# Products of one-query attention issued in register-addressed loops instead of written out

## The chip, the cores and the metric

One NeuronCore of a Trainium2 chip runs the whole program. The time is device microseconds of one execution, taken as the median of three executions. A profile of one execution gives the span from the first to the last instruction and the records that the text below reads.

## The reference, cut to what matters

One token attends to 65,536 cached positions in 16 heads of 256 values; a small gated layer multiplies the result. All tensors are bf16.

```python
# x (1,1,448); k_cache, v_cache (1,16,65536,256); wq (448,4096); wo (4096,448); w1 (448,1792); w2 (1792,448)
xn = layernorm(x)
q = (xn @ wq).reshape(1, 1, 16, 256).transpose(0, 2, 1, 3)
scores = einsum("bhqd,bhkd->bhqk", q, k_cache) * 256 ** -0.5
p = softmax(scores)
o = einsum("bhqk,bhkd->bhqd", p, v_cache)
s = o.transpose(0, 2, 1, 3).reshape(1, 1, 4096) @ wo
g = silu(silu(xn @ w1) @ w2)
out = x + s * g
```

Keys and values together are 1,074 MB; each byte is used once.

## The kernel before, in words

**Blocks and buffers.** The cache is cut into 64 blocks (`NBLK`), four for each head. A block is 16,384 positions: 128 partitions, each with `KB` = 128 positions of 256 values, 8.39 MB. Three such buffers in SBUF (`R[0]` to `R[2]`, one tensor `RR`) hold keys and values in turn: slot `s` takes the keys of block i, then the values of block i, then the keys of block i + 3. SyncE's queue (SP) issues all loads in the order keys(i), values(i - 1), keys(i + 1), values(i), and so on. In `load_k` (L227) it first takes the semaphores `vh[s]` and `vf[s]`, which TensorE raises when the values in that slot have been multiplied, half and whole; in `load_v` (L233) it takes `kf[s]`, which VectorE raises when the keys in that slot have been used.

**Scores.** VectorE (`dve_block`) multiplies the keys by the query and sums part of the products itself; ScalarE (`act_sums`, L331) sums the other part, 18 of each 32 positions, in four steps for a block (`SUB` = 32). VectorE's `end` needs both. It copies the scores (L261) and takes the maximum of each partition (L262, semaphore `rm`).

**Values.** TensorE runs `pe_block` for each block: `pe_turn` (turns the previous result, needs `oc`), `pe_max` (maximum over partitions, next query, broadcast: L378, L440, L384) and `pe_v` (L452), which multiplies the values of the block before that maximum's. `pe_v` accumulates 64 products of two positions each, 128 x 512 values a product (L366 in `pe_keys`), in the two rows of `psO`, and raises `od`; the one-column product of `pe_mark` (L450) then raises `vf[s]`. ScalarE, in the middle of its own next block (after two of four steps), takes `od` and copies `psO` to `O` (`act_out`, L357), which raises `oc`; a step later it stores the turned result (`act_row`, L361).

**Order at the two ends.** The first blocks wait for their data. In the last ones, block 61's values go through `pe_v_split`: 96 positions (most of them in a loop of four register-addressed products, L464 and L466), then `pe_max` of block 62, then the rest. Block 62's values come in two pieces and block 63's in three; both are multiplied by `pe_groups` (L408), which spreads the products over four pairs of rows in one PSUM bank, 32 rows apart, and needs `pe_turn_groups` (L422) and a VectorE sum (`dve_row`, L434) behind it. Between these stand the maxima of the last keys, and the output projection (`project`, L928) by pieces of `wo` that come last of all loads. The gate's second `silu` on ScalarE (L722) and VectorE (L724 to L731), the weights of the last head (L869 to L879) and the final sum over blocks (L888, L895) run on those engines in program order.

The outer TensorE loop, three blocks a pass, is written with the helper `loop`. Two queues, SP's and ScalarE's, store the two halves of the output (L1036).

Of the kernel before, what the change touches and what calls it, by code (L numbers as in the profile page):

```python
# [10 lines left out]
ET = mybir.EngineType  # L11
# [3 lines left out]
KB = 128  # L15
SUB = 32
NR = 3
# [7 lines left out]
def kernel(  # L25
# [12 lines left out]
    nc = tc.nc  # L38
    bf16 = mybir.dt.bfloat16
    fp32 = mybir.dt.float32  # L40
    P = nc.NUM_PARTITIONS

    _, _, D = A_x.shape
    _, H, Sk, Dh = A_k_cache.shape
# [4 lines left out]
    NBLK = H * NB  # L49
    assert NBLK % NR == 1 and NBLK >= 8  # L50
    LAST = NBLK - 1
# [19 lines left out]
    pe, dve, act, gp, sp = nc.tensor, nc.vector, nc.scalar, nc.gpsimd, nc.sync  # L71


    KW, HK = KB * Dh, KB // 2
# [8 lines left out]
    PVV = pool.tile([P, NR * KB], bf16, name="PV")  # L83
# [10 lines left out]
    hist = pool.tile([P, 2 + NENT, 4], fp32, name="hist")  # L94
    ident = pool.tile([P, P], bf16, name="ident")
# [28 lines left out]
    wq_t, n = rest(0, DF * HD + HD // 2)  # L124
    Z, n = rest(n, DX * HP * HP)
    w1_t, n = rest(n, DF * F + F // 2)
    w2_t, n = rest(n, FC * D)
# [35 lines left out]
    def mark(e, ins):  # L163
        count[e] += 1
        ins.then_inc(line[e], 1)
        return (e, count[e])

    def need(e, *toks):
        for p, c in toks:
            if seen.get((e, p), 0) < c:  # L170
                eng[e].wait_ge(line[p], c)
                seen[(e, p)] = c
# [4 lines left out]
    def take(e, s, k=1):  # L177
        e.wait_ge(s, k).then_inc(s, -k)  # L178
# [176 lines left out]
    def act_out(po=psO):  # L355
        take(act, od)
        act.copy(out=O[0 : po.shape[0], :], in_=po).then_inc(oc, 1)  # L357

    def act_row(e):
        take(act, ho)  # L360
        return act.copy(out=hist[:, at(e + 2), 2:4].rearrange("p o s -> p (o s)"), in_=ps_t)  # L361


    def pe_keys(po, t, s, k0, k1, start, stop, done=None):
        for c in range(k0, k1, 2):
            ins = pe.matmul(  # L366
                po,
                lhsT=PV[t][:, c : c + 2],
                rhs=R[s][:, c * Dh : (c + 2) * Dh],
                start=(start and c == k0),  # L370
                stop=(stop and c == k1 - 2),
            )
        if done is not None:
            ins.then_inc(done, 1)

    def pe_rows():
        take(pe, rm)
        pe.matmul(  # L378
            ps_m[0:1, :], lhsT=rmax[:, 0:1], rhs=ident[:, :], start=True, stop=True
        ).then_inc(tm, 1)  # L380

    def pe_bcast():
        take(pe, gm)
        pe.matmul(  # L384
            ps_nb, lhsT=ones_row[0:1, :], rhs=gmax[0:1, :], start=True, stop=True
        ).then_inc(bm, 1)
# [3 lines left out]
    def pe_turn():  # L390
        take(pe, oc)
        Ov = O[0:2, :].rearrange("r (j p a) -> r j a p", j=2, a=2)
        for a in range(2):
            for j in range(2):
                ins = pe.matmul(  # L395
                    ps_t2[:, 2 * a : 2 * a + 2],
                    lhsT=Ov[:, j, a, :],
                    rhs=eye2[:, j, :],
                    start=(j == 0),
                    stop=(j == 1),  # L400
                    is_transpose=True,
                )
        ins.then_inc(ho, 1)

    def pe_groups(po, t, s, k0, k1, first, end):
        for c in range(k0, k1, 2):
            p = PG * (c // 2 % G)
            ins = pe.matmul(  # L408
                po[p : p + 2, :],
                lhsT=PV[t][:, c : c + 2],  # L410
                rhs=R[s][:, c * Dh : (c + 2) * Dh],
                start=(c < first + 2 * G),
                stop=(c >= end - 2 * G),
            )
        return ins

    def pe_turn_groups():
        take(pe, oc)
        Ov = O[:, :].rearrange("r (j p a) -> r j a p", j=2, a=2)
        for a in range(2):  # L420
            for j in range(2):
                ins = pe.matmul(  # L422
                    ps_tg[:, a, :],
                    lhsT=Ov[:, j, a, :],
                    rhs=eye4[:, j, :],
                    start=(j == 0),
                    stop=(j == 1),
                    is_transpose=True,
                )
        return mark("pe", ins)  # L430

    def dve_row(o, t):
        need("dve", t)
        return mark("dve", dve.tensor_reduce(out=o, in_=ps_t4, axis=AX.X, op=ALU.add))  # L434
# [14 lines left out]
    def pe_mark():  # L449
        return pe.matmul(ps_z, lhsT=ident[:, 0:1], rhs=ident[:, 0:1], start=True, stop=True)  # L450

    def pe_v(s):  # L452
        take(pe, pv)
        take(pe, vl[s], 16)
        pe_keys(psO, s, s, 0, HK, True, False, vh[s])
        pe_keys(psO, s, s, HK, KB, False, True, od)
        pe_mark().then_inc(vf[s], 1)

    def pe_v_split(s, k, between):
        take(pe, pv)  # L460
        take(pe, vl[s], 16)
        n = SUB // 4
        pe_keys(psO, s, s, 0, n, True, False)
        with nc.Fori(n, k, n, engines={ET.PE}, hint_back_edge=True) as c:  # L464
            for d in range(0, n, 2):
                pe.matmul(  # L466
                    psO,
                    lhsT=PVV[:, bass.ds(c + (s * KB + d), 2)],
                    rhs=RR[:, bass.ds(c * Dh + (s * KW + d * Dh), 2 * Dh)],
                    start=False,  # L470
                    stop=False,
                )
        between()
        pe_keys(psO, s, s, k, KB, False, True, od)
        pe_mark().then_inc(vf[s], 1)


    def pe_max(i):
        pe_rows()
        pe_query(i + 1)  # L480
        pe_bcast()

    def pe_block(i, s):
        pe_turn()
        pe_max(i)
        pe_v(s)
# [4 lines left out]
    def loop(g, a, b, step, block, more=0, always=False):  # L491
        es, name = {g.engine}, f"passes_{nc.next_id()}"
        head, ann, body, rest, join, tail = (
            f"{name}_{x}" for x in ("head", "ann", "body", "rest", "join", "tail")
        )
        assert (b - a) % step == 0 and more < step
        last = b if more else b - step
        r = nc.alloc_registers(f"{name}_i", engines=es)
        nc.regs_mov(r, a)
        nc.br(head, engines=es)  # L500

        def go(lo, hi):
            i = nc.snap(r, min_val=a, max_val=last)
            for s in range(lo, hi):
                block(i + s, s)

        if always:
            with nc.body(head, valid_engines=es):
                hint = g.mark_branch_hint_location()
                nc.br(body, engines=es)  # L510
        else:
            with nc.body(head, valid_engines=es):
                g.br_eq(r, last, on_true=body, on_false=ann)
            with nc.body(ann, valid_engines=es):
                hint = g.mark_branch_hint_location()
                nc.br(body, engines=es)
        with nc.body(body, valid_engines=es):
            go(0, more or step)
            if more:
                g.br_eq(r, last, on_true=join, on_false=rest)  # L520
            else:
                nc.br(join, engines=es)
        if more:
            with nc.body(rest, valid_engines=es):
                go(more, step)
                nc.br(join, engines=es)
        with nc.body(join, valid_engines=es):
            nc.regs_alu(r, r, step, op=mybir.AluOpType.add)
            g.br_lt(r, last + 1, on_true=head, on_false=tail).branch_hint(hint)
        nc.switch_bb(tail)  # L530
# [76 lines left out]
    with tc.tile_critical(sync_engine=ET.Pool, no_gpsimd_drain=True):  # L607
# [228 lines left out]
        none(ps_t2).then_inc(ho, 1)  # L836
        need("pe", t9)
        pe_max(0)
        loop(pe, 1, NBLK - 3, NR, pe_block, more=1)
        pe_turn()  # L840
        pe_v_split(1, 96, lambda: pe_max(NBLK - 2))


        def shares(e0, e1, h0, h1):
# [115 lines left out]
        take(pe, pv)  # L960

        pe.wait_ge(nl[0], 16)
        pe_groups(ps_g, 2, 2, 0, HK, 0, KB)
        pe_rows()
        pe_bcast()
        pe_quads()
        pe.wait_ge(nl[1], 16)
        pe_groups(ps_g, 2, 2, HK, KB, 0, KB).then_inc(od, 1)
        take(pe, wy)
        pe.wait_ge(wp, 16)  # L970
        project(0, 4 * PQ)
        take(pe, pv)
        pe.wait_ge(zl[0], 16)
        pe_groups(ps_g2, 0, 1, 0, HK, 0, HK).then_inc(od, 1)
        act_out(ps_g)
        act_softmax(LAST + 1, PV[0][:, HK:KB], HK, KB)
        pe_rows()
        pe.wait_ge(wl[0], 16)
# [1 line left out]
        project(r0, r1 - 2)  # L980
        pe_bcast()
        project(r1 - 2, r1)
        t = pe_turn_groups()
        need("act", t)
        act_out(ps_g2)
        t = dve_row(hist[:, LAST + 1, 2:4], t)
        t = mark("dve", dve.memset(g_t, 0.0))
        mark("dve", dve.memset(x_t, 0.0))
        need("dve", ("dve", count["dve"]))
        for p, w in halves:  # L990
            mark("dve", dve.tensor_copy(out=x_t[p, :], in_=x_f[0:1, w]))
        t_g = silu([(g_t[p, :], w) for p, w in halves], ps_y, g_e, t_y)
        need("pe", t)
        t_x = pe_turn_groups()
        take(pe, pv)
        t15 = pe_sums(ps_m[:, 0:NL], N1, NENT)
# [5 lines left out]
        need("dve", t)  # L1002
        weights(N1, NENT, H1, H, (ps_m[:, 0:NL], t15))
        t_r = dve_row(hist[:, LAST + 2, 2:4], t_x)
        need("dve", t_r)
        outputs(N1, NENT - 1, H1, H, NL - 1)
        for n in range(1, len(vz)):
            pe.wait_ge(zl[n], 16)
# [58 lines left out]
```

## Time and profile before

| | before |
|---|---|
| median of three runs (lowest to highest) | 2513.66 us (2513.61 to 2513.69) |
| the profiled execution's own time | 2513.66 us |
| its span, first to last instruction | 2511.3 us |
| VectorE busy | 2175.9 us, 87% of the span |
| ScalarE busy | 1930.3 us, 77% |
| TensorE busy | 1129.9 us, 45% |
| moved by DMA | 1084.37 MB, 432 GB/s over the span |
| mean granted TensorE clock | 0.702 |

The profiled execution took as long as the median of the runs, so its rows can be set against the measured time directly; 2.4 us of the time lie outside the span. In the profile's lines, PE is TensorE, PEld its weight loads, DVE VectorE, ACT ScalarE and SP SyncE; a letter q behind an engine means its sequencer. L366 is a line of the kernel file. In a timeline, the columns are start in us, length in us, engine, line, operation, output from inputs and count; in brackets stands how long the engine had been idle before and what ended that.

### The profile page before, as it was taken

To read this page: it belongs to the slowest core of one execution; us is meant where nothing else is said; L and a number is where in the kernel's file an instruction comes from. 1 tells how busy PE (TensorE), PEld (TensorE's weight loads), DVE (VectorE), ACT (ScalarE), POOL (GpSimd) and SP (SyncE) were. 2 spreads that over 40 slices of the span, in tenths; PEclk is the share of its full clock that TensorE was granted. 3 is DMA by queue.
4 is the path that set the end of the run, shared out by engine and by line. 5 is a ranking of instruction groups with operands and counts; after the bars stand their busy time and mean duration, and the time that the engine had idled before them with its cause. 6 is when DMAs were issued, how large, how long until landed. Compare 5 with 4: busy or idle time off the path is not lost. (4 is left out here: it accounts for less than half of the span.)

```text
span 2511.3 us, 30167 instructions
## 1 busy us (share of the span) xinstructions
PE 1129.9 (45%) x4775; PEld 430.3 (17%) x4775; DVE 2175.9 (87%) x1573; ACT 1930.3 (77%) x9555; POOL 2.4 (0%) x17
## 2 busy tenths in 40 slices
PE   3253543534535445345354453443544534435455
PEld 1121211211112112111121121111211211112122
DVE  6979889889898898898988988989889888898898
ACT  5868778778787787787877877878778777787786
POOL 0000000000000000000000000000000000000000
PEclk7676766767667677677676776766767767677677
DMA  9999999999999999999999999999999999999999
GB/s 424 424 437 434 434 434 434 434 433 434 431 433 432 432 433 434 430 433 434 434 434 433 434 434 434 434 434 434 434 434 434 431 433 432 434 433 432 431 431 386
DMA packets 21738, 1084.37 MB, mean 432 GB/s; under 512 B 2405, under 2 KB 2918, under 8 KB 3942
## 3 DMA queue, kind: packets, MB, share of 16 engines
q1 hardware_dynamic: 21730, 1084.30, 99.9%
q8 instruction: 4, 0.07, 0.0%
q10 hardware_dynamic: 4, 0.00, 0.0%
HBM read 1084.29 MB, written 0.00 MB: 432 GB/s over the span
## 5 line engine op out<-in xcount | busy, mean ns | idle before, releaser
L331 ACT ACTIVATE R<-R x4608 | 1839.0, 400 | 368.6 <-ACTq L178 368.6
L268 DVE TENSOR_TENSOR R<-R,qcur 128x4608 bf16<-128x4608 bf16 (+1 forms) x512 | 1130.9, 2219 | 248.5 <-DVEq L178 248.4
L366 PE MATMUL bank<-R,PV 128*2 128x512 bf16 x3924 | 985.9, 418 | 13.3 <-PEq L178 5.8
L314 DVE TENSOR_REDUCE S<-R 128x13 f32<-128x3328 bf16 (+1 forms) x256 | 925.8, 3617 | 0.0
L331 ACT ACTIVATION_READ_ACCUMULATOR R<-R x4608 | 857.4, 186 | 0.0
L366 PEld LDWEIGHTS bank<-R,PV 128*2 128x2 bf16 x3924 | 351.4, 90 | 620.7 <-issue 203.5
L378 PE MATMUL bank<-ident,rmax 128*1 128x128 bf16 x65 | 17.2, 264 | 931.0 <-PEq L178 930.8
L395 PE MATMUL bank<-eye,O 2*128 2x2 f32 x252 | 38.2, 252 | 379.1 <-PEq L178 379.1
L378 PEld LDWEIGHTS bank<-ident,rmax 128*1 128x1 bf16 x65 | 5.2, 79 | 936.5 <-issue 936.5
L344 ACT ACTIVATE hist<-bank 128x1 f32 (+1 forms) x65 | 11.1, 171 | 157.5 <-ACTq L178 157.5
L302 DVE CUSTOM_DVE_ANT_0 R<-R,qcur 128x256 bf16<-128x256 bf16 x252 | 105.4, 418 | 0.0
L395 PEld LDWEIGHTS bank<-eye,O 2*128 2x128 f32 x252 | 34.6, 208 | 395.5 <-issue 395.5
L250 DVE TENSOR_REDUCE gmax<-bank 1x1 bf16<-1x128 f32 x65 | 18.3, 281 | 35.9 <-DVEq L178 35.9
L357 ACT COPY O<-bank 2x512 f32<-2x512 f32 (+1 forms) x67 | 37.5, 560 | 6.8 <-ACTq L178 6.6
L289 DVE CAST qcur<-bank 128x256 bf16<-128x256 f32 x64 | 27.2, 425 | 16.0 <-DVEq L178 15.9
L346 ACT ACTIVATE PV<-S,hist 128x128 f32 (+1 forms) x65 | 26.0, 400 | 14.7 <-ACTq L178 14.4
L440 PE MATMUL bank<-q,ident 8*128 (+1 forms) x63 | 24.3, 386 | 7.6 <-issue 1.2
L261 DVE COPY S<-S 128x128 f32<-128x128 f32 (+1 forms) x65 | 14.7, 226 | 11.7 <-DVEq L178 2.5
L408 PE MATMUL bank<-R,PV 128*2 128x512 bf16 x128 | 13.9, 604 | 15.4 <-DMA R<-in_A_v_cache_dram 15.4
L302 DVE DVE_READ_ACCUMULATOR2_ANT S<- 128x1 f32 x252 | 20.8, 82 | 0.0
L262 DVE TENSOR_REDUCE rmax<-S 128x1 bf16<-128x128 f32 (+1 forms) x65 | 18.2, 280 | 0.0
L384 PE MATMUL bank<-gmax,ones_row 1*128 1x1 bf16 x65 | 10.3, 158 | 6.9 <-PEq L178 2.9
(90 smaller groups left out, 133.8 us busy)
## 6 DMA issues: line engine op xcount, KB each, us to landing
R<-in_A_k_cache_dram SPq DMA_DIRECT2D x7, 4096.0 KB, 26.5
R<-in_A_v_cache_dram SPq DMA_DIRECT2D x3, 4096.0 KB, 24.6
R<-in_A_k_cache_dram SPq DMA_DIRECT2D x2, 2048.0 KB, 19.9
R<-in_A_wq_dram SPq DMA_DIRECT2D x1, 3072.0 KB, 12.8
R<-in_A_v_cache_dram SPq DMA_DIRECT2D x1, 3072.0 KB, 23.0
R<-in_A_wo_dram SPq DMA_DIRECT2D x4, 448.0 KB, 26.6
R<-in_B_w_dram SPq DMA_DIRECT2D x1, 1568.0 KB, 25.3
R<-in_B_w_dram SPq DMA_DIRECT2D x1, 1344.0 KB, 5.7
```

Of the source, the lines that this page charges most:

```text
L250: dve.reduce_max(out=gmax[0:1, :], in_=ps_m[0:1, :], axis=AX.X).then_inc(gm, 1)
L268: return dve.tensor_tensor(out=keys, in0=keys, in1=qcur[:, None, :].to_broadcast([P, c1 - c0, Dh]), op=ALU.mult,)
L289: dve.tensor_copy(out=qcur[:, :], in_=ps_q).then_inc(sd, 1)
L302: dve.tensor_tensor_reduce(out=Kv[:, c, :], in0=Kv[:, c, :], in1=qcur[:, :], scale=1.0, scalar=0.0, op0=ALU.mult, op1=ALU.add, accum_out=S ...
L314: ins = dve.tensor_reduce(out=S[:, c1:c2], in_=Kv[:, c1:c2, :], axis=AX.X, op=ALU.add)
L331: ins = act.activation(out=prod, in_=prod, func=ACT.Identity, accum_out=S[:, bass.ds(c0 + c, 1)],)
L346: act.activation(out=pv_out, in_=S2[:, c0:c1], func=ACT.Exp, bias=col(0, 1), scale=scale, accum_out=col(1, 2),).then_inc(pv, 1)
L357: act.copy(out=O[0 : po.shape[0], :], in_=po).then_inc(oc, 1)
L366: ins = pe.matmul(po, lhsT=PV[t][:, c : c + 2], rhs=R[s][:, c * Dh : (c + 2) * Dh], start=(start and c == k0), stop=(stop and c == k1 - 2),)
L378: pe.matmul(ps_m[0:1, :], lhsT=rmax[:, 0:1], rhs=ident[:, :], start=True, stop=True).then_inc(tm, 1)
L395: ins = pe.matmul(ps_t2[:, 2 * a : 2 * a + 2], lhsT=Ov[:, j, a, :], rhs=eye2[:, j, :], start=(j == 0), stop=(j == 1), is_transpose=True,)
L440: pe.matmul(ps_q, lhsT=ident[0:HP, at(j)].to_broadcast([HP, P]), rhs=q8[:, o : o + Dh] if isinstance(o, int) else q8[:, bass.ds(o, Dh)], s ...
```

## The change

The TensorE code for the values is rewritten. `pe_keys_loop` multiplies positions k0 to k1 in a loop of four products a pass (8 positions), with the addresses of weights and data taken from the loop's register. `pe_zero` is a product of 128 x 512 with a zero result that opens and closes the accumulation, since the products in the loop neither start nor stop it. `pe_v` is now: zero, loop over one half, a `pe_mark` that raises `vh[s]`, loop over the other half, zero, mark. Block 61 uses the same function with `pe_max` between. Block 62's values, which used `pe_groups`, now go through the loop too, in pieces of 32, 32 and 64 positions, into the two rows of `psO`; so their result is turned by `pe_turn` and stored by ScalarE's `act_row` in place of VectorE's `dve_row`. Block 63 keeps `pe_groups`. The outer loop of TensorE is an ordinary `Fori`, with one block behind it. The two stores of the output are the same in both kernels.

```diff
-    def pe_v(s):
-        take(pe, pv)
-        take(pe, vl[s], 16)
-        pe_keys(psO, s, s, 0, HK, True, False, vh[s])
-        pe_keys(psO, s, s, HK, KB, False, True, od)
-        pe_mark().then_inc(vf[s], 1)
-
-    def pe_v_split(s, k, between):
...
-        pe_keys(psO, s, s, 0, n, True, False)
-        with nc.Fori(n, k, n, engines={ET.PE}, hint_back_edge=True) as c:
+    def pe_keys_loop(t, s, k0, k1):
+        n = 8
+        with nc.Fori(k0, k1, n, engines={ET.PE}, hint_back_edge=True) as r:
+            c = nc.snap(r, min_val=k0, max_val=k1 - n)
             for d in range(0, n, 2):
                 pe.matmul(
                     psO,
-                    lhsT=PVV[:, bass.ds(c + (s * KB + d), 2)],
+                    lhsT=PVV[:, bass.ds(c + (t * KB + d), 2)],
                     rhs=RR[:, bass.ds(c * Dh + (s * KW + d * Dh), 2 * Dh)],
                     start=False,
                     stop=False,
                 )
-        between()
-        pe_keys(psO, s, s, k, KB, False, True, od)
+
+    def pe_zero(start):
+        return pe.matmul(
+            psO,
+            lhsT=ident[:, 0:2],
+            rhs=ident[:, 2:3].to_broadcast([P, 2 * Dh]),
+            start=start,
+            stop=not start,
+        )
+
+    def pe_v(s, k=HK, between=None):
+        take(pe, pv)
+        take(pe, vl[s], 16)
+        pe_zero(True)
+        pe_keys_loop(s, s, 0, k)
+        if between:
+            between()
+        else:
+            pe_mark().then_inc(vh[s], 1)
+        pe_keys_loop(s, s, k, KB)
+        pe_zero(False).then_inc(od, 1)
         pe_mark().then_inc(vf[s], 1)
...
-        loop(pe, 1, NBLK - 3, NR, pe_block, more=1)
+        with nc.Fori(1, NBLK - 3, NR, engines={ET.PE}, hint_back_edge=True) as i:
+            for s in range(NR):
+                pe_block(i + s, s)
+        pe_block(NBLK - 3, 0)
         pe_turn()
-        pe_v_split(1, 96, lambda: pe_max(NBLK - 2))
+        pe_v(1, 96, lambda: pe_max(NBLK - 2))
...
         pe.wait_ge(nl[0], 16)
-        pe_groups(ps_g, 2, 2, 0, HK, 0, KB)
+        pe_zero(True)
+        pe_keys_loop(2, 2, 0, SUB)
         pe_rows()
+        pe_keys_loop(2, 2, SUB, HK)
         pe_bcast()
         pe_quads()
         pe.wait_ge(nl[1], 16)
-        pe_groups(ps_g, 2, 2, HK, KB, 0, KB).then_inc(od, 1)
+        pe_keys_loop(2, 2, HK, KB)
+        pe_zero(False).then_inc(od, 1)
...
-        act_out(ps_g)
+        act_out()
...
-        t = pe_turn_groups()
-        need("act", t)
+        pe_turn()
+        t_a = mark("act", act_row(LAST - 1))
         act_out(ps_g2)
-        t = dve_row(hist[:, LAST + 1, 2:4], t)
...
-        need("pe", t)
+        need("pe", t_a)
         t_x = pe_turn_groups()
...
-        need("dve", t_r)
+        need("dve", t_a, t_r)
```

More of the change, by code (lines that the diff above doesn't have):

```diff
@@ L450, in pe_mark @@
         return pe.matmul(ps_z, lhsT=ident[:, 0:1], rhs=ident[:, 0:1], start=True, stop=True)
-    def pe_v(s):
-        take(pe, pv)
-        take(pe, vl[s], 16)
-        pe_keys(psO, s, s, 0, HK, True, False, vh[s])
-        pe_keys(psO, s, s, HK, KB, False, True, od)
-        pe_mark().then_inc(vf[s], 1)
-    def pe_v_split(s, k, between):
-        take(pe, pv)
-        take(pe, vl[s], 16)
-        n = SUB // 4
-        pe_keys(psO, s, s, 0, n, True, False)
-        with nc.Fori(n, k, n, engines={ET.PE}, hint_back_edge=True) as c:
+    def pe_keys_loop(t, s, k0, k1):
+        n = 8
+        with nc.Fori(k0, k1, n, engines={ET.PE}, hint_back_edge=True) as r:
+            c = nc.snap(r, min_val=k0, max_val=k1 - n)
             for d in range(0, n, 2):
```

## The prediction

> **What bounds the kernel now.** First the page: share of the DMA engines, queues, and the chain that ended last.
>
> ```profile
> DMA  9999999999999999999999999999999999999999
> ...
> q1 hardware_dynamic: 21730, 1084.30, 99.9%
> q8 instruction: 4, 0.07, 0.0%
> ...
> DMA R<-in_A_wo_dram 1%; SPq L810 0%; SPq L237 0%; PE bank L928 0%; DVE S L1031 0%; DVE S L1033 0%
> ```
>
> The 16 DMA engines never rest, and the last load ends the program. At 433 GB/s a block (16.8 MB of keys and values) takes 38.7 us, and that is the period of every engine's work. The change moves no byte, so it can cost time only where a load is issued too late or where the work after the last loads grows. Hence the second view, the timeline of one steady block:
>
> ```profile
> 2300.51 0.33 SPq L233 DMA_DIRECT2D R<-in_A_v_cache_dram  x1
> ...
> 2301.80 15.77 PE L366 MATMUL bank<-R,PV 128*2 128x512 bf16 x64 [0.21 <-PEq L178]
> ...
> 2308.68 0.42 ACT L331 ACTIVATE R<-R  x1 [5.99 <-ACTq L178]
> ...
> 2317.85 0.33 SPq L227 DMA_DIRECT2D R<-in_A_k_cache_dram  x1
> ...
> 2323.06 0.56 ACT L357 COPY O<-bank 2x512 f32<-2x512 f32 x1
> ```
>
> TensorE's 64 products (call their stretch V, first product to mark: 15.6 us here, 15.1 to 16.8 over the blocks) hold two things: the next load of keys (2317.85) and ScalarE's copy of the result (2323.06). Values issued at 2300.51 land after a median 24.6 us, at 2325.1; until then the DMA engines are busy without the keys.
>
> Third, the price of a looped product. Block 61 already runs in such a loop (timeline of TensorE, then the loop's own line):
>
> ```profile
> 2443.08 7.37 PE L466 MATMUL bank<-R,PV 128*2 x28
> 2450.68 1.02 PE L466 MATMUL bank<-R,PV 128*2 x4 [0.23 <-issue]
> 2451.87 1.02 PE L466 MATMUL bank<-R,PV 128*2 x4 [0.17 <-issue]
> 2453.12 1.02 PE L466 MATMUL bank<-R,PV 128*2 x4 [0.23 <-issue]
> 2454.37 1.02 PE L466 MATMUL bank<-R,PV 128*2 x4 [0.23 <-issue]
> ```
>
> ```profile
> L464 PEldq BRANCH_PREFETCH_HINT  x11: 31/31/35, 2441.6 to 2454.1; - x11
> ...
> L464 PEldq COMPARE_BRANCH  x11: 80/230/240, 2442.6 to 2455.0; - x11
> ```
>
> Eleven passes begin from 2441.6 to 2454.1: 1.25 us a pass. While the clock is still low (a product each 0.43 us) the array is slower than that; after it rises (0.215 us) four products take 0.86 us and the array waits for its sequencer in each pass ("issue"). So the sequencer sets the pace.
>
> **The change, part by part.** *V of blocks 0 to 60.* 16 passes x 1.25 = 20.0 us; 0.1 us to enter the first loop and 0.15 for mark and entry of the second (in the trace the wait's end to the first hint is 0.2 us, eight more instructions included); 0.2 for the closing zero. V = 20.5. The second `snap` adds a register move per pass that no row shows alone. Joined to the register instruction already there (L464, 78 ns; the smallest of this kind is 42) it costs little; alone it costs 0.1 us, as the MOVE at 2441.46 before the hint at 2441.56. I take 0.02, nearer to the joined row: 0.3 us a block, with ends 0 and 1.6. Below nothing: some passes take 1.20. So V = 20.8, between 19.7 and 22.1, or 4.9 us more than the mean of 15.9.
>
> [...] The profile shows four instruction packets in all, and the trace has none between 66 and 2434 us, while TensorE's outer loop jumped back some twenty times; so the jumps are put at nothing.
>
> *Who waits for a longer V.* Two limits.
> (a) The load of keys. From V's start (2301.80) to the landing of the values ahead (2325.1) are 23.3 us. Off go 0.45 from the mark to the issue and 1.05 from issue to first packet (the run's first DMA: issued at 0.90, first packet at 1.95). V may reach 21.8.
> (b) ScalarE. It works without a gap through its block (only the 5.99 us at its start are idle), and the copy stands in its middle. Where the copy does wait, at the start, TensorE and ScalarE make a loop of their own (timelines of TensorE and ScalarE):
>
> ```profile
> 98.71 16.50 PE L366 MATMUL bank<-R,PV 128*2 128x512 bf16 x64 [3.30 <-PEq L178]
> 115.05 0.17 PE L450 MATMUL bank<-ident 128*1 128x1 bf16 x1
> ...
> 132.38 4.85 PE L366 MATMUL bank<-R,PV 128*2 128x512 bf16 x11
> ```
>
> ```profile
> 115.33 0.57 ACT L357 COPY O<-bank 2x512 f32<-2x512 f32 x1 [2.25 <-ACTq L178]
> ```
>
> From the mark (115.05) to the next V (132.38) are 17.3 us: copy, second half of the sums, maximum, next query. So the loop needs V + 17.3 a block and fits into 38.7 while V stays below 21.4. With 20.8 both limits hold: no cost in steady state, 0.6 us to spare.
>
> *The start.* V of block 0 begins with its landing (98.71) and ends 4.4 us later than before; ScalarE, already waiting there, goes 4.3 us late, and with it VectorE and V of block 1: 136.7 instead of 132.4. Its mark comes at 157.5, the keys' issue 0.3 later (149.25 before), their first packet at 158.8; the values ahead land at 157.8 (issued 130.99, now some 4 us later, still in time). The engines rest about 1.0 us, once; block 2's V comes at 174.8 by (b), and from block 3 on the loads lead again. Ends 0 and 3.
>
> *The tail.* Timelines of ScalarE, TensorE and VectorE:
>
> ```profile
> 2460.12 0.57 ACT L357 COPY O<-bank 2x512 f32<-2x512 f32 x1 [2.55 <-ACTq L178]
> ```
>
> ```profile
> 2470.46 3.58 PE L408 MATMUL bank<-R,PV 128*2 128x512 bf16 x32 [9.02 <-DMA R<-in_A_v_cache_dram]
> 2476.22 0.27 PE L378 MATMUL bank<-ident,rmax 128*1 128x128 bf16 x1 [2.17 <-PEq L178]
> ...
> 2480.76 3.58 PE L408 MATMUL bank<-R,PV 128*2 128x512 bf16 x32
> ```
>
> ```profile
> 2496.89 2.94 DVE L728 RECIPROCAL R<-R 1x448 f32<-1x448 f32 x1
> ```
>
> - Block 61: twelve looped passes before `pe_max` (now at 2456.6, +1.3), then four: result at 2463.2 instead of 2460.0. ScalarE's copy, which already waits there, goes 3.2 later and with it all its sums of the last block, VectorE's first half (L261 at 2478.5, +2.8) and its second (rm at 2496.1, +2.8).
> - Block 62: `pe_groups` took 3.6 us for 32 products; the loop takes 5.0 for 16. TensorE: four passes from 2470.5, `pe_rows` at 2479.0 (waits for rm), four passes to 2484.2, broadcast, quads, eight passes to 2494.5, result 2495.0 (before 2484.3). Then `project` to 2495.8, block 63's first half (3.5) to 2499.3, `pe_rows` at 2499.3 instead of 2493.4: +5.9.
> - From there the chain is that of before plus `pe_turn` and `act_row`: broadcast 2500.1, turn 2501.1, row 2501.35, ScalarE's copy to 2501.9, `silu` (L722) 2501.9 instead of 2495.9. VectorE's 2.94 us reciprocal and what follows it end the sum over blocks at about 2508.6 (before 2502.68); this took the place of the loads as what is last. The final `pe_turn_groups` needs `t_r` (2508.2, before 2502.28): 2508.4 to 2509.1; in its row, the remaining projections (28 products x 0.05, then 4) end at 2510.6 instead of 2507.85.
>
> The loads, which end at 2507.5, hid 5.9 us only to the extent of 3.1. Tail: +2.8, with ends 1 and 6 (a longer pass counts 28 times; cold products after waits add some tenths).
>
> **Sum.** The profiled execution took 2513.66, as the median of the runs. 0 in steady state + 1.0 + 2.8 + 0.5 for entries, exits and cold products that I don't see singly = +4.3: 2518.0. A measurement of this kernel can tell about 0.2% (5.0 us) from no change, and this lies just within.
>
> **Rivals.**
> 1. *ScalarE's copy becomes the bound (slower).* If V exceeds 21.4, by a lone move in each pass or dearer entries, every block from about 3 to 60 pays the excess: at 22.1, 0.7 x 57 = 40 us, 2558. For it: only 0.6 us to spare, and both limits lie together. Against it: the measured pass of the same body. Chance 0.15.
> 2. *The array's clock falls within the loop*, as the array rests 0.2 to 0.4 us a pass. At 0.43 us a product V would be 27 us, the excess 6 x 57: 2855. Against it: in block 61 products after five such passes still come at 0.215. Chance 0.02.
> 3. *Nothing is seen:* the tail stays under the last loads and the start loses nothing: 2514.5. For it: the loads hid the old tail. Against it: the reciprocal stands in program order behind a result 5.9 us late. Chance 0.10.
> 4. *Faster:* a shorter program could only save instruction packets, four in all, 0.07 MB or 0.2 us of DMA, and the stores are unchanged. Over 0.2% there is no room: 1084 MB at 433 GB/s are 2504 us, and of the span of 2511 another 2 lie before the first packet and 4 behind the last load's. Chance 0.02.
>
> My forecast has the remaining 0.71; its terms spread from +2 to +9, about 0.40 of it under +5.0 and 0.31 above. With rival 3 on the one side and rivals 1 and 2 on the other: faster 0.02, same 0.5, slower 0.48. The range 2514.2 to 2532 leaves out rival 2, most of rival 1 above 18 us, and the lowest part of rival 3.
>
> **What would show it.** V of 20.5 to 21.1 in steady blocks, with four products and a gap in each 1.25 us; keys issued about 1.9 us before the values ahead land; ScalarE's copy idle only at the start and the end; DMA at 433 GB/s from 200 to 2440 us; one short dip near 158 us; the chain that ended last through L728 and L434 instead of DMA. Wrong, if ScalarE waits at L357 in every block, if a pass takes over 1.3 us, or if the last DMA still ends the chain.

## The result, and the profile after

| | before | after |
|---|---|---|
| median (lowest to highest), six runs each | 2513.68 us (2513.58 to 2514.19) | 2548.09 us (2538.34 to 2558.29) |
| the profiled execution's own time | 2513.66 us | 2542.66 us |
| its span | 2511.3 us | 2540.8 us |

The ratio is 1.0137, interval 1.011 to 1.0163: the change costs 34 us, or 29 us in the execution that was profiled. The page of after: DMA rate by slices, queues, the chain that ended last, and two groups.

```profile
GB/s 422 428 437 430 428 429 426 427 431 429 428 415 429 427 426 428 431 420 442 432 428 430 429 430 429 431 427 430 426 427 417 431 422 432 430 427 427 418 428 383
...
q1 hardware_dynamic: 21730, 1084.30, 99.5%
q8 instruction: 3, 0.05, 0.0%
...
PE bank L941 0%; PE bank L422 0%; DVE S L1046 0%; DVE S L1048 0%
...
L457 PE MATMUL bank<-R,PV 128*2 x4032 | 1093.6, 413 | 99.2 <-issue 84.7
...
L357 ACT COPY O<-bank 2x512 f32<-2x512 f32 (+1 forms) x67 | 37.4, 559 | 10.0 <-ACTq L178 10.0
```

The bytes are the same, and no stage stands out: the median rate of a slice is 428, with 31 of 40 slices between 426 and 432, where 433 was forecast. The loss is spread over the whole run. ScalarE's copy (L357) waited 10.0 us in all before its 67 executions (6.8 in before), so the copy did not become the bound. Program fetch is three packets. The chain now ends in products and vector sums instead of a load.

One steady block of after, by the timeline:

```profile
957.68 0.59 PE L466 MATMUL bank<-ident 128*2 128x512 bf16 x1
...
958.19 9.64 PE L457 MATMUL bank<-R,PV 128*2 x32
...
967.67 0.17 PE L450 MATMUL bank<-ident 128*1 128x1 bf16 x1
...
968.01 1.02 PE L457 MATMUL bank<-R,PV 128*2 x4 [0.17 <-issue]
...
969.20 1.02 PE L457 MATMUL bank<-R,PV 128*2 x4 [0.17 <-issue]
...
970.45 1.02 PE L457 MATMUL bank<-R,PV 128*2 x4 [0.22 <-issue]
...
977.48 0.38 PE L466 MATMUL bank<-ident 128*2 128x512 bf16 x1
...
977.69 0.17 PE L450 MATMUL bank<-ident 128*1 128x1 bf16 x1
...
978.14 0.33 SPq L227 DMA_DIRECT2D R<-in_A_k_cache_dram  x1
...
979.01 0.56 ACT L357 COPY O<-bank 2x512 f32<-2x512 f32 x1
```

V runs from 957.68 to the mark at 977.69: 20.0 us, four products and a gap of 0.2 us in each 1.24 us. The keys are issued 0.45 later, and ScalarE's copy at 979.01 follows its neighbours without a gap. The values ahead of these keys had been issued at 956.43. The time from issue to landing of the two loads, by the DMA view of that stretch:

```profile
R<-in_A_v_cache_dram SPq DMA_DIRECT2D x1, 24.6
R<-in_A_k_cache_dram SPq DMA_DIRECT2D x1, 23.7
```

The values landed at 981.05, so the keys were issued 2.9 us ahead of that landing, which the prediction held to be ample. Yet they landed at 1001.85, 20.8 us behind the values. In before, every load of keys landed 19.35 us behind the values ahead of it. This one lost 1.45 us. The 112 loads from the landing at 215.73 to the one at 2410.91 took 2195.2 us; the same loads took 2167.3 in before. The difference, 27.9 us, is nearly all of the span's 29.5.

The packet records of the trace, which the views above sum up, show how. Each load is spread over 16 DMA engines in 128 packets of 64 KB. The records name no engine; a packet is counted to the engine whose last packet ended just before it. In before, a packet takes 2.42 us, none of the engines is ever idle between 220 and 2420 us, and they don't end a load together: the first one ends its share 2.43 us before the load's landing (2.0 us before the last engine's last packet, which ends 0.4 before the landing). In after, engines run dry before the keys' packets come: between 220 and 2420 us the 16 engines idle 9.8 us each more than in before, and 788 of the run's 15,616 packets of 64 KB take more than 2.5 us. Of these slow packets 478 start within 4 us behind an issue of keys; half of the 478 take over 2.8 us, a third 3.0 or more (the longest 4.3). Idle and slow packets cost some 30 us an engine together.

### The profile page after: what moved, and what is told of

It reads as the page before. It is cut to its first block, busy times and chain, and to the rows that moved or that the text cites. A ratio compares the mean times of both kernels' runs of the same rounds, so it can differ in the third digit from the quotient of the medians.

```text
span 2540.8 us, 38241 instructions
## 1 busy us (share of the span) xinstructions
PE 1260.5 (50%) x4962; PEld 437.7 (17%) x4962; DVE 2175.7 (86%) x1572; ACT 1930.5 (76%) x9556; POOL 2.4 (0%) x17
## 3 DMA queue, kind: packets, MB, share of 16 engines
q1 hardware_dynamic: 21730, 1084.30, 99.5%
## 5 line engine op out<-in xcount | busy, mean ns | idle before, releaser
L457 PE MATMUL bank<-R,PV 128*2 x4032 | 1093.6, 413 | 99.2 <-issue 84.7
L457 PEld LDWEIGHTS bank<-R,PV 128*2 x4032 | 348.4, 87 | 824.1 <-issue 558.8
L466 PE MATMUL bank<-ident 128*2 128x512 bf16 x126 | 60.8, 482 | 18.2 <-DMA R<-in_A_v_cache_dram 6.5
L357 ACT COPY O<-bank 2x512 f32<-2x512 f32 (+1 forms) x67 | 37.4, 559 | 10.0 <-ACTq L178 10.0
L450 PE MATMUL bank<-ident 128*1 128x1 bf16 x123 | 20.6, 168 | 0.0
L262 DVE TENSOR_REDUCE rmax<-S 128x1 bf16<-128x128 f32 (+1 forms) x65 | 18.2, 280 | 0.0
```

The lines of the kernel that those rows point to most:

```text
L457: pe.matmul(psO, lhsT=PVV[:, bass.ds(c + (t * KB + d), 2)], rhs=RR[:, bass.ds(c * Dh + (s * KW + d * Dh), 2 * Dh)], start=False, stop=False,)
L466: return pe.matmul(psO, lhsT=ident[:, 0:2], rhs=ident[:, 2:3].to_broadcast([P, 2 * Dh]), start=start, stop=not start,)
```

## Theories and experiments

**A**: the keys are issued too late, and the DMA engines run dry although the values ahead have not landed. **B**: the prediction's sum (start and tail), with little in the steady blocks. **C**: looping disturbs the transfers in some other way. Later **A2**: the loss grows in proportion to the delay. "Idle products" in the edits are products of 128 x 512 into an unused bank.

### 1. Written out again

After's program, with only the steady `pe_v` written out; the loops of the last blocks and the new tail stay.

```diff
+        if between is None:
+            pe_keys(psO, s, s, 0, HK, True, False, vh[s])
+            pe_keys(psO, s, s, HK, KB, False, True, od)
+            pe_mark().then_inc(vf[s], 1)
+            return
         pe_zero(True)
         pe_keys_loop(s, s, 0, k)
...
```

> The changed kernel with the products of blocks 0 to 60 written out again; the loops remain for blocks 61 and 62 and so does the new tail. Theory A (the keys' load is issued too late once V is 20 us long, and some of the 16 DMA engines run dry at each such load): V back to 15 to 17 us, keys issued 6 to 8 us before the values ahead land, every load of keys lands 19.36 us after the values; only the tail's cost is left, 2514 to 2518 us. Theory B (the prediction's sum: the loss sits in the tail and the start): nearly all of the loss stays but for the start's 1 us, 2540 or more.

Measured: 2513.93 us (2513.18 to 2515.65), ratio 1.0000 (0.9991 to 1.001). Every load of keys landed 19.35 us behind its values. So the loss sits in the steady loop, and the tail that the prediction priced at 2.8 us costs less than 1 us: the median span is 2512.1 us, 0.7 above before's. Single executions lose more behind the steady blocks: the profiled one, the slowest of the ten (2515.65), lost 2.4 us in the loads that landed after 2383 us.

### 2. Late without a loop

Before's program, with 19 idle products between the result's semaphore and the mark. The steady blocks hold no loop of products; only the keys' issue (and nothing that ScalarE needs) comes later, at 19.2 to 20.9 us.

```diff
         pe_keys(psO, s, s, HK, KB, False, True, od)
+        for _ in range(19):
+            pe.matmul(
+                bank[6][0:2, :],
+                lhsT=ident[:, 0:2],
+                rhs=ident[:, 2:3].to_broadcast([P, 2 * Dh]),
+                start=True,
+                stop=True,
+            )
         pe_mark().then_inc(vf[s], 1)
```

> The kernel before, all products written out, with 19 idle products of 512 columns into an unused bank between the raising of od and the mark that releases the keys' slot (19 x 0.215 = 4.1 us), blocks 0 to 60. ScalarE's copy is released as before. Theory A: keys are issued 2.1 to 3.8 us before the values ahead land and this alone costs as much as the change or more, 2540 to 2560 us, with first packets of keys of 3.0 to 3.6 us in place of 2.42. Theory C (the register-addressed loop itself disturbs the transfers, by its reads or its fetching of program): nothing is looped here, so 2513 to 2516 us.

Measured: 2550.52 us (2544.7 to 2555.2), ratio 1.0153 (1.0136 to 1.017). The loop is not needed for the loss; a late mark is enough. The time from issue to landing of all keys (us), in before, in after and then in this kernel:

```profile
DMA to landing us min/median/max: 25.5/26.4/45.4
```

```profile
DMA to landing us min/median/max: 22.3/24.0/42.8
```

```profile
DMA to landing us min/median/max: 22.0/23.3/44.1
```

A shorter time here means a shorter queue ahead at the issue: the load that is issued latest waits least, and that is the bad sign.

### 3. Idle products behind the mark

The same 19 products, one line lower.

```diff
         pe_mark().then_inc(vf[s], 1)
+        for _ in range(19):
+            pe.matmul(...)
```

> Control for e2: the kernel before with the same 19 idle products a block, but behind the mark that releases the keys, so that keys are issued 6 to 8 us ahead as before; od is raised before them, too. If e2's loss came from the late keys: 2513.5 to 2515 us. If the idle products themselves disturbed the transfers: 2540 or more.

Measured: 2513.86 us (2513.62 to 2514.36), ratio 1.0001 (0.9991 to 1.001). The same 19 products that cost 37 us ahead of the mark cost 0.2 us behind it: what they delay is what matters here.

### 4. Loop kept, mark earlier

After's program with eight products a pass.

```diff
-        n = 8
+        n = 16
```

> The changed kernel with eight products a pass in place of four. From the rows, a pass of four takes 1.24 us, of which each product takes 0.15 us and the loop's own instructions 0.63, so a pass of eight should need 1.87 us of the sequencer and 1.72 us of the array: V of 16 to 17 us. Theory A: keys in time again, 2514 to 2518 us. Theory B: 2540 or more, less some 1 us for shorter loops in the tail.

Measured: 2513.27 us (2513.06 to 2515.01), ratio 1.0000 (0.999 to 1.0009), with V of 15.6 to 17.2 in the steady blocks and keys issued 5.7 to 7.4 us before the values land. Its chain, and the loop's own line (passes; shortest, median, longest in ns):

```profile
DMA R<-in_A_wo_dram 1%; SPq L820 0%; PE bank L941 0%; SPq L237 0%; DVE S L1046 0%; DVE S L1048 0%
```

```profile
L454 PEldq COMPARE_BRANCH  x504: 80/227/249, 98.9 to 2488.6; - x168
```

Half the 1008 jumps at the same price each (227 ns at the median, 225 in after), and the array, not its sequencer, sets the pace again: in the block whose mark stands at 1002.24 us the last 29 looped products fill one row of the timeline (995.65, 6.54 us). The chain ends with a load as in before. C falls: looped products with register addresses cost nothing here. This is also the version to keep: as fast as before, with only four more products written out in each loop than after has.

### 5. How late is too late

The edit of experiment 2 with 10, 13 and 28 idle products.

> As e2 and e5, with 10 idle products (2.2 us). In the runs so far a load of keys lost time where the first of the 16 engines came to the end of its share of the values less than 1.5 us after the issue (0.8 to 1.2 us on the average), and 0.1 or less where it came later, however far ahead of the last engine's landing that was. Here the first engine ends 23.3 - 2.4 - 0.45 - 18.1 = 2.4 us after the issue, 1.6 to 3.2 over the blocks. By that rule nothing is lost, 2513.5 to 2516 us; by a loss in proportion to the delay (e5 lost 19 us with 13 products), 2528 us.

> As e2, with 13 idle products in place of 19 (2.8 us): keys issued 3.4 to 5.0 us before the values ahead land. From the loads of keys in the changed kernel and in e2, those issued over 3.3 us ahead took 0.0 to 0.1 us more than 19.35, those under it 0.5 to 2.1. Theory A with this bound: nothing is lost, 2513.5 to 2516 us. If instead every delay of the keys costs in proportion (a rival, A2: any shorter lead slows the transfers a little), 13/19 of e2's loss, 2539 us.

> As e2, with 28 idle products (6.0 us): without any loss keys would be issued 0.2 to 1.9 us before the values ahead land. A loss at one load of keys delays the values behind it but not the release of the next slot, so it buys the next load as much lead; the pattern should settle where lead = 1.0 + loss, with the losses of 2.1 us at a lead of 2 to 2.5 seen in e2: some 1.6 us at each of 59 loads, 2590 to 2640 us, about 2610. The prediction's own limit (the last engine to finish must find its next packet, 1.05 us after issue) would give only 0 to 0.9 us a load, on the average 0.3: 2530 us.

| idle products | time (us) | ratio (interval) |
|---|---|---|
| 10 | 2515.76 (2514.56 to 2520.85) | 1.001 (1.0 to 1.0019) |
| 13 | 2533.16 (2528.13 to 2535.22) | 1.007 (1.0053 to 1.0087) |
| 19 | 2550.52 (2544.7 to 2555.2) | 1.0153 (1.0136 to 1.017) |
| 28 | 2573.2 (2569.1 to 2574.87) | 1.0233 (1.0216 to 1.025) |

The share of the 16 engines' span that packets took, with 10 and with 28 products:

```profile
q1 hardware_dynamic: 21730, 1084.30, 99.8%
```

```profile
q1 hardware_dynamic: 21730, 1084.30, 98.6%
```

Neither a bound of 3.3 us before the landing nor A2 holds. Ten products cost almost nothing where A2 has 2528. Thirteen cost 19 us, and loads with 3.3 to 4.0 us of lead to the landing lost 0.7 us on average. With 28, loads with 2.5 to 3.3 us of lead lost nothing (0.07 at most). What orders all of them is another count: from the issue to the moment when the *first* of the 16 engines ends its share of the values. Loads of keys of after and of the runs with 13, 19 and 28, by that lead (the two in three for which the landing of the values ahead is on record):

| first engine ends, us behind the issue | loads | mean loss, us |
|---|---|---|
| under 1 | 61 | 1.0 to 1.2 |
| 1 to 1.5 | 14 | 0.78 |
| 1.5 to 2 | 12 | 0.08 |
| 2 to 4 | 65 | 0.03 |

With 28 products the time from the first engine's end to the landing had shrunk from 2.4 to about 1 us; there a lead of 3 us to the landing is 2 us to the first engine. This explains why those loads lost nothing. The bound was read from these four runs; the 10-product run was forecast by it, and came out so. From 13 products on the time grows with each product by 2.5 to 2.9 us, where 57 loads of keys at 0.215 would be 12: what one load loses, the next has as additional lead. This last step is argued, not tested.

### 6. Keys in two loads

After's program; the first half of the keys is issued as soon as `vh` allows it, the second behind `vf`.

```diff
-        take(sp, vf[s])
-        sp.dma_start(out=R[s][:, :], in_=block(Kd, i)).then_inc(kl[s], 16)
+        if h is None:
+            take(sp, vf[s])
+        load_keys(R[s], block(Kd, i), 0, HK, kl[s])
         sp.sem_inc(kq[s], 16)
-        sp.sem_inc(kh[s], 16)
+        if h is not None:
+            take(sp, vf[s])
+        load_keys(R[s], block(Kd, i), HK, KB, kh[s])
```

> The changed kernel with all its loops; only the keys' load is cut in two: the first half of a slot is loaded when vh says that its first half of values is multiplied, the second half when vf does. Theory A: the first half is issued some 13 us before the values ahead land, the second waits behind it in the queue, no engine runs dry, 2514 to 2519 us. Theory C: the loops are as they were, so 2538 to 2558 us.

Measured: 2518.53 us (2517.84 to 2518.87), ratio 1.0019 (1.0009 to 1.0028). No engine idles any more (packets take 99.9% of the 16 engines' span, 99.5 in after), with after's loop as it is. Nearly all of the remaining 4.8 us is in the loads of keys: halves mean packets of 32 KB, and keys land 19.43 instead of 19.35 us behind the values, 57 times 0.08, or 4.6. But the first half was issued a median 22.8 us ahead of the values' landing, not 13, and the second 12.8: the whole chain of work had moved forward by some 10 us, which the next experiment explains. The early release by `vh` alone is not tested by this run.

### 7. Are smaller packets the cure?

Experiment 6 changes lead and packet size at once. Two controls take the halves and issue both late. The first:

```diff
         take(sp, vf[s])
-        sp.dma_start(out=R[s][:, :], in_=block(Kd, i)).then_inc(kl[s], 16)
+        load_keys(R[s], block(Kd, i), 0, HK, kl[s])
         sp.sem_inc(kq[s], 16)
-        sp.sem_inc(kh[s], 16)
+        load_keys(R[s], block(Kd, i), HK, KB, kh[s])
```

> Control for e3: the changed kernel with the keys cut into two loads as there, but both issued only when the whole slot is free (vh and vf), so as late as in the changed kernel. If e3 was cured by the early issue of its first half: the loss is back, 2540 to 2560 us. If it was cured by the smaller loads or packets: 2518 us as e3.

Measured: 2518.76 us (2517.7 to 2520.55), ratio 1.002 (1.001 to 1.003). As a control it failed: `kl` now rises with the first half, VectorE begins its block 9.7 us earlier, and everything behind it, the values' products too; the same holds for experiment 6. Keys were issued 12.8 to 14.5 us ahead of the landing in the steady blocks; they were not late. The second control loads the halves in the other order, so that VectorE starts no earlier:

```diff
-        sp.dma_start(out=R[s][:, :], in_=block(Kd, i)).then_inc(kl[s], 16)
+        load_keys(R[s], block(Kd, i), HK, KB, kh[s])
+        load_keys(R[s], block(Kd, i), 0, HK, kl[s])
         sp.sem_inc(kq[s], 16)
-        sp.sem_inc(kh[s], 16)
```

> The control that e9 did not give: there VectorE began on a block when its first half had landed, 9.7 us earlier, so TensorE's V too came earlier and the keys went out 12.8 to 14.5 us ahead, late or not. Here the two halves are issued in the other order, the second half of the positions first, and VectorE can begin only with the last one: the chain and the lead are those of the changed kernel (2.9 us where V is 20.0), with two loads of 32 KB packets. If the lead alone decides: the loss is back, 2540 to 2562 us. If a late load loses only with 64 KB packets, or as one load: 2518 us.

Measured: 2558.25 us (2555.21 to 2559.5), ratio 1.0173 (1.0156 to 1.019). Its queue:

```profile
q1 hardware_dynamic: 30370, 1084.31, 99.3%
```

The keys were issued 3.0 to 6.6 us ahead of the landing (2.9 to 6.8 in after). With the same packets as experiment 6, the loss is back. Lead is the cure, not packet size.

### 8. Values in two loads

If the stagger of the engines came from the size of the packets ahead, halving the values' packets would shrink it and save the late keys.

```diff
-        sp.dma_start(out=R[s][:, :], in_=block(Vd, i)).then_inc(vl[s], 16)
+        load_keys(R[s], block(Vd, i), 0, HK, vl[s])
+        load_keys(R[s], block(Vd, i), HK, KB, vl[s])
...
-        take(pe, vl[s], 16)
+        take(pe, vl[s], 32)
```

> The changed kernel with its late keys, but each block of values is loaded by two DMAs, issued together, in packets of 32 KB in place of 64. If the lead that keys need is one packet's time of the 16 engines' stagger (2.42 us) plus about 1 us from issue to first packet, then with packets half as long it falls from 3.4 to some 2.2 us, the keys' 2.9 us suffice, and what is left is the tail and the smaller packets' own cost (4 us over the run, as e3's loads show): 2517 to 2523 us. If the lead is a fixed time, or the stagger stays what it is since it is handed on from load to load, the loss stays: 2538 to 2560 us.

Measured: 2548.63 us (2546.48 to 2549.09), ratio 1.0138 (1.0121 to 1.0155): as after. The time from the first engine's end to the landing stayed at a median of 2.40 us, so the halves did not shrink it, and what would happen with a smaller one isn't answered by this run.

### 9. The other limit: ScalarE's loop

Before's program: the mark stands right behind the products, so that the keys stay early, and the result's semaphore comes 32 idle products later.

```diff
-        pe_keys(psO, s, s, HK, KB, False, True, od)
+        pe_keys(psO, s, s, HK, KB, False, True)
         pe_mark().then_inc(vf[s], 1)
+        for _ in range(32):
+            pe.matmul(...)
+        pe_mark().then_inc(od, 1)
```

> The kernel before, with the mark that releases the keys right behind the products, as before, but od, which releases ScalarE's copy, raised only after 32 more idle products of 512 columns (6.9 us). The prediction's limit (b): TensorE and ScalarE need 15.9 + 6.9 + 17.3 = 40.1 us a block, 1.4 over the loads' 38.7, so 58 x 1.4 = 81 us more, 2595 (2570 to 2620). If ScalarE can take up the delay in the 6 us that it idles at the start of a block, nothing: 2514.

Measured: 2652.33 us (2650.2 to 2653.07), ratio 1.0551 (1.0534 to 1.0569). Its timeline:

```profile
1037.47 16.79 PE L366 MATMUL bank<-R,PV 128*2 128x512 bf16 x64
...
1054.55 0.33 SPq L227 DMA_DIRECT2D R<-in_A_k_cache_dram  x1
...
1061.09 0.17 PE L450 MATMUL bank<-ident 128*1 128x1 bf16 x1
...
1061.37 0.57 ACT L357 COPY O<-bank 2x512 f32<-2x512 f32 x1 [6.42 <-ACTq L178]
```

Now ScalarE waits at its copy, 6.42 us in this block. From the first product to the result's mark are 1061.09 - 1037.47 = 23.62 us, and the next block's products begin at 1078.43: a period of 40.96 = 23.62 + 17.34. The prediction's formula, V + 17.3, is exact. The time came out above the expected one because its V was taken as 22.8.

## Why the prediction was wrong, by its own steps

**V: right for two blocks in three.** Forecast 20.8 (19.7 to 22.1); measured 20.0 in two of three blocks and 18.2, below the range, in the third. The loop's lines, then its products' line:

```profile
L454 PEldq FUSED_REGOPS  x1008: 84/84/84, 97.4 to 2521.2; - x168
...
L454 PEldq COMPARE_BRANCH  x1008: 80/225/244, 98.2 to 2522.1; - x168
```

```profile
L457 PEldq FUSED_REGOPS  x3696: 42/74/85, 97.6 to 2521.8; - x195
```

The second `snap` went into the register instruction already there (84 ns instead of 78), as taken. The branch costs 225 ns at the median, near the row shown, 230. Unforeseen: 4032 products need 3696 register operations, 336 fewer. Those are one a pass for the 21 blocks in slot 0, whose offset is zero, and the sequencer's passes there take 1.13 us (1050.16 to 1051.28) instead of 1.24.

**Limit (a), the load of keys: the step that failed.** The prediction let V reach 21.8 by counting up to the landing of the values, less 0.45 to the issue and 1.05 to the first packet. A landing comes behind the end of the last of 16 engines (0.4 us in before); the first runs out 2.4 us before it, and did so in before's packet records too. And 1.05 us to the first packet is not enough: loads issued 1 to 1.5 us ahead of the first engine's end still lost 0.78 us on average. The limit by these numbers is 23.3 - 2.4 - 0.45 - 1.5 = 18.9 us. V at 18.2 stays below it, V at 20.0 does not, and the loads divide in the same way: the 37 loads of keys behind a V of 20.0 lost 26.1 us, 0.7 each on average, the 19 behind a V of 18.2 lost 0.8 in all. The sum's 0 for the steady state was 27.9 us. The prediction saw 1.0 us to spare under this limit (0.6 under limit (b)) where 1.1 were missing. Its own check, "keys issued about 1.9 us before the values land" (2.05 by its own terms, 23.3 - 20.8 - 0.45), came out kinder (2.9 or more), and the loss came all the same.

From issue to first packet the rows have 0.97 us at the steady issue of 741.65 us (first packet behind it at 742.62), or 0.64 from the end of the issuing instruction, which takes 0.33, and 1.5 are needed to lose nothing. Behind that issue the first eight packets of keys took 3.0 to 3.6 us instead of 2.42; no run here shows the cause.

**Limit (b), ScalarE: right.** It was not reached (L357 idle 10.0 us in all), and experiment 9 confirms its formula. Rival 1 (2558 us) comes near the measured time, but by a mechanism that did not occur.

**The start: forecast +1.0, measured 0.** V of block 0 began 1.5 us sooner than in before (97.20; the loads there land 1.5 us sooner, the keys issued at 34.89 at 77.68 instead of 79.22) and took 18.2 us (slot 0), so V of block 1 began at 132.79, not 136.7; the keys behind it left at 153.44 instead of 157.8, with 4.2 us of lead to the landing at 157.66, and landed 19.36 us behind it.

**The tail: forecast +2.8, measured +0.6.** From the last load's landing to the final product on VectorE (L1046; L1031 in before) were 0.36 us before and are 0.96 now (2536.46 to 2537.42). Block 63's first half in before, then TensorE's and VectorE's timelines of after:

```profile
2489.89 3.50 PE L408 MATMUL bank<-R,PV 128*2 128x512 bf16 x32 [3.61 <-DMA R<-in_A_v_cache_dram]
```

```profile
2522.69 0.44 PE L408 MATMUL bank<-R,PV 128*2 128x512 bf16 x3
...
2522.91 1.95 PE L408 MATMUL bank<-R,PV 128*2 128x512 bf16 x29
...
2533.69 0.90 PE L422 MATMUL bank<-eye,O 98*128 98x98 f32 x4 [1.09 <-PEq L178]
2534.52 2.42 PE L941 MATMUL bank<-R,OTq 128*32 128x224 bf16 x24
2536.73 0.64 PE L941 MATMUL bank<-R,OT 128*32 128x224 bf16 x8
```

```profile
2528.20 2.94 DVE L738 RECIPROCAL R<-R 1x448 f32<-1x448 f32 x1
...
2533.42 0.17 DVE L434 TENSOR_REDUCE hist<-bank 128x2 f32<-128x8 f32 x1
...
2537.42 0.38 DVE L1046 TENSOR_TENSOR S<-bank,q 33x224 bf16<-33x224 f32 x1 [2.29 <-PE bank L941]
```

The path is the one forecast: reciprocal, L434, L422, projections. Its sizes differ in both directions. Block 63's first half took 2.2 us, not 3.5: the 32 products now follow looped ones without a rest, at 0.07 us each and a granted clock of 1.00; in before they followed 3.61 us of waiting for their load, at 0.11 and a clock of 0.53. It also began 13.8 us before the last landing where the forecast had 11.7 (2495.8 to 2507.5). These two are most of why L422 began 2.8 us before the last landing (2533.69), where the forecast had it 0.9 us behind (2508.4 to 2507.5). The 32 projections behind it then took 2.85 us, not 1.5. The entries and exits put at +0.5 are not seen singly; what is left of 29.5 - 27.9 - 0.6 is 1.0 us, lost in the loads behind 2411 us.

**Program fetch and clock: right.** Three instruction packets with the 1008 jumps of the products' loops, a mean granted clock of 0.741 (0.702 in before), and products in the loop that follow each other at 0.215 us within a pass. Program fetched for the jumps, put at nothing, does not show in this trace.

## What to carry to other kernels

In these runs, where one queue had to keep 16 DMA engines busy, a load's deadline was not the landing of the one ahead: it was the end of the first engine's share (2.4 us earlier), less a margin (1.5 us). The first can be read in the packet records of a trace without any idle time. The margin can't, and the time to a first packet (1.05 us) was too small a stand-in; it took runs with the load issued late. When work that was off the critical path gets longer, list every semaphore that it raises and find the one whose waiter feeds the bound; here a loop of eight products (experiment 4) gives it all back.

## What the runs showed of the hardware

- DMA engines that had run dry were slow to take up again: behind the issue of keys at 978.14 us ten of the first sixteen 64 KB packets took 2.9 to 3.7 us instead of 2.42, and in some loads the last of the 16 engines to begin did so up to 1.7 us after the load ahead had ended on all of them. Why stays open.
- 8.4 MB of keys in 32 KB packets land 0.08 us later than in 64 KB packets (19.43 to 19.35 us).
- Four register-addressed products of 128 x 512 a pass were bound by the sequencer (1.24 us a pass, with the array idle 0.2 of it); with eight the array had no such gaps (V of 15.6 to 17.2 us, 15.1 to 16.8 written out).
- Profiled executions with the rewritten last blocks (after and experiments 1, 4, 6, 7 and 8) have 1.8 to 1.9 us outside their span, those with before's 2.3 to 2.4, with or without idle products. It explains experiment 4's 0.4 us under before; its cause was not looked for.
